# Linear attention and a gated feed-forward layer: loads of v and DMA transposes apart, the last block's addition ahead of its seventh product, new lists for blocks 2 to 8

## The chip, the cores and the metric

The kernel runs on one core of one Trainium2 chip. The metric is the device time of a run in microseconds (us), of which the median of three runs is given. A profile is one execution that the hardware profiler recorded; it has a time of its own, and all stretches, gaps and durations below are measured from the start of its span.

The engines are called PE or TensorE (matmul; PEld is its weight load), DVE or VectorE, ACT or ScalarE, POOL or GpSimd, and SP or SyncE, which here only issues DMAs. L12 is line 12 of the kernel before.

## What is computed

Attention without a score matrix: softmax of q over the head dimension, softmax of k over the sequence, and two small products. The result is laid out as 4608 rows of 512 and goes through a feed-forward layer with a GELU gate.

```python
def _attn_ref(q, k, v):             # each (8, 8, 576, 64): batch, heads, sequence, head dimension
    q_s = softmax of q over its last axis
    k_s = softmax of k over the sequence
    kv = np.einsum('bhsd,bhse->bhde', k_s, v)
    return np.einsum('bhsd,bhde->bhse', q_s, kv)

def _moe_ref(x, w_gate, w_val, w_out):   # x (4608, 512), w_gate and w_val (512, 1536), w_out (1536, 512)
    gelu = 0.5 * g * (1.0 + erf(g / sqrt(2)))     # g = x @ w_gate
    return (gelu * (x @ w_val)) @ w_out
```

## The kernel before, in words

**Blocks.** One batch element is one block. Of its 576 rows 512 are worked through with the block; the 64 that are left of each element are gathered in `xtr` and make up a block of their own, number 8, which comes ahead of the last one. So the order is 0 to 6, 8, 7. While block b goes through its feed-forward layer, the attention of the next one is made beside it.

**Attention of one block.** q, k and v come by two DMAs each on SyncE's queue (`load`, L180). ScalarE makes the exponentials of q and k (`exp`, L223, instruction at L227). VectorE sums those of q and takes reciprocals (`norm_pair`, L250), and GpSimd multiplies (L265). The normalised `eq` is transposed by a DMA on SyncE's queue (`unit_td`, L415, DMA at L418) into `eqt`. v is cast to 16 bits by ScalarE or GpSimd (`cast_v`, L232). TensorE makes kv from the exponentials of k and v (`unit_kv4`, L361), VectorE normalises it (`kv4_norm`, L374), TensorE multiplies it with `eqt` (`unit_x4`, L454), and ScalarE and VectorE copy one half each of the result to `xt` (`x4_out`, L484). From block 3 on, `eq` has one buffer: the exponentials of the next q are written to where the transpose reads.

**Feed-forward layer.** From block 2 on all its matrix products are done by Strassen's scheme with seven products of half size. `product_gv` (L660) makes one product of the first layer for one of six column groups (0, 1, 2, 6, 7, 8), value and gate together: four matmuls of 128x256. `product` (L739) makes one of the seven products of the second layer, twelve matmuls of 128x256. Which sums of x, h and the weights they need is in `sum_x` (L653), `sum_h` (L616) and `sum_w1` (L644). Several products share a PSUM bank: product 1, then 6, then 7, then 4 of the second layer add up in `psA`, product 5, then 3, in `psC`, and product 2 in `psB`. Between two of them another engine must have read the bank: y1 is read from `psA` after product 1, y2 after product 6, y5 from `psC` after product 5. The additions b+ (`psB` and y1), c+ (`psC` and y2) and a+ (`psA` and y5) make three quarters of the block's output, and the last quarter is `psA` after product 4.

**What sets the order.** Nothing is scheduled by the compiler. `PROG` (L675) holds a list of entries for each block from 2 on, and `play` (L817) issues them one after another; every engine works through its own in that order. The entries that the text speaks of:

- `0P1`: product 1 of the first layer, column group 0 (the digit in front). `0c`: ScalarE copies product 1 to the bank of the other sum. `0s2`, `0s5`: scale a bank's content into SBUF (ScalarE; with d, VectorE). `0a2`, `0a5`: VectorE's additions. `0g2`, `0g4`: GELU on ScalarE. `0m2`, `0m4`: VectorE's multiplication with the gate. `0u`: GELU of the other half. `0U`: its multiplication on GpSimd, `0Ud` on VectorE.
- `s01p`, `s21d`: sums of h, on GpSimd (p) or VectorE (d). `x0d`, `x1p` and so on: sums of x. `z`: the same for the last block. `w`: sums of weights.
- `O1:03`: product 1 of the second layer, its steps 0 and 3. `O7`: product 7. `y1a`, `y2d`: y1 by ScalarE, y2 by VectorE. `b+`, `c+`, `a+`: the additions. `yea`: the last quarter, by ScalarE. c+ and ye are each followed by a store of 512 KB.
- `lq`, `lk`, `lv`: the loads for two blocks on. `Eq`, `Ek`: exponentials of q and k. `NA`, `NB`: sums and reciprocals. `M0` to `M3`: GpSimd's multiplications. `t`: the transpose. `tr`: a small transpose for the rows of block 0 in block 8. `V0a` to `V3p`: casts of v. `K`, `k`, `X`, `Xa`, `Xd`: kv, its normalisation, the product with `eqt`, and its two copies. `TE`, `TG`: ScalarE's table for the exponential or for GELU.
- `<` in front of an entry means that it belongs to the block before, `>` to the one after.

A DMA waits on SyncE's sequencer for what it needs, and all DMAs behind it on that queue wait with it.

**The last block.** Its output banks are split in two, one for each 128 rows. `finish_last` (L962) makes product 7 for the first half, its addition (L965), the same for the second half, stores the second half's columns, makes product 4 for the first half (read by ScalarE, L970, and stored from ScalarE's queue), and for the second half (read by VectorE, L973, and stored from SyncE's). It is called at `O7`; `c+` of that block, with its 512 KB store, comes behind it in the list.

Of the kernel before, what the change touches and what calls it, by code (L numbers as in the profile page):

```python
# [18 lines left out]
def kernel(  # L19
# [640 lines left out]
    def product_gv(i, ps, xt, k, first):  # L660
        lo, hi = slice(k * P, (k + 1) * P), slice((k + NO // 2) * P, (k + NO // 2 + 1) * P)
        xs = xs_b[xt is st.get((B - 1, "xt"))]
        for t, w, nm in ((0, wv_sb, "v"), (1, wg_sb, "g")):
# [9 lines left out]


    PROG = {  # L675
        2: ("lk lq lv 6P1 0P1 <x0p 2P1 w81d 0P5 <x1d 6P5 <x3d 6c w82d 6P2 0c <x2d 6P6 w71d 0s5 0P6 6s5 0P3 6P3 6s2 "
            "w72p 6g2 0P2 NB 0s2 6P7 6m2 w83p 0P7 0g2 6a2 1P1 2c 0a2 2P2 M3 1P5 0a5 1c 0P4 0m2 2g2 1P2 0u 6a5 M2 1P6 "
            "0g4 2P5 6u 2P6 1s5 0U 6P4 1g2 NA 1P3 1s2 0m4 2m2 1P7 2s5 6U 1m2 7P1 2s2 2P3 6g4 1a2 s01p 2P7 1a5 7P5 6m4 "
            "1u 1P4 2a2 M0 8P1 7c 2a5 7P6 7s5 w73d 7P2 w74d 8c 8P5 7s2 1Ud 7P3 1g4 w84d 8P6 s02d 2u 7P7 s04d 8s5 2P4 "
            "7a2 8s2 8P3 7a5 2U 8P7 2g4 1m4 8P2 7u 8a2 7P4 7g2 M1 t O1:03 8g2 >>lr 8a5 8P4 7g4 2m4 7m2 O1:1 8u O1:4 "  # L680
            "7U 8m2 O1:25 8g4 7m4 K 8m4 8U O2 s11d TE s21d y1a s23d s22d O5 s24d s12d k O6 Eq b+ s14p y5a O3:03142 "
            "s03p y2a >NB X s13d O7 Xa Xd O3:5 x0d"),
        3: ("0P1 <x1d 6P1 <a+ 0P5 <O4 <c+ <x3p <Ek lk 6c 0c 6P5 M2 lq 0s5 6P6 NA 0P3 6s5 M3 0P6 <yea 6s2d 0P2 6P3 "
            "<x2p 0s2d 6P2 <TG 0P7 0a2 0g2 1P1 M1 6a2 <V3a 6P7 6g2 <V2p 0a5 7P1 1c 6m2 0P4 0u 1P5 6a5 7c 1P6 0Ud 0g4 "
            "1P2 6u 1s5d 6P4 1s2 7P2 6Ud 1P3 0m2 1P7 0m4 7g2 6g4 7P5 7m2 s01p 7P6 <V1a 1a5 2P1 7s5 6m4 1P4 M0 7s2 1a2 "
            "7P3 1g2 s02d 7P7 1g4 1m2 8P1 2c s04d 1m4 2P6 <V0a 2P5 lv 7a5 8c O1:03 7a2 2s2 O1:1 t 7P4 1u 8P6 7u 2P7 "
            "1Ud 2s5 8P5 8s2 2P3 7g4 2a5 8P7 7U 8s5 2P2 2a2 8P2 s11p 8P3 2g2 8a5 7m4 8P4 8g2 2P4 s13p 2u 8a2 O1:4 8g4 "
            "K 8m2 2g4 8m4 O2 2m4 8u 2U 2m2 8Ud s21d O1:25 TE s23d O5 s12d s14d y1a s22d O6 k b+ s24p y5d X Eq >lq "
            "s03p O3:03142 y2a V3p Xd O7 Xa V0a"),
        4: ("6P1 NA 0P1 <x0d <O3:5 <x1d 6P5 0P5 <a+ <Ek lk <O4 0c <c+ <x3p 6c 0s5d <V2p 0P6 6P6 <TG 0P3 M0 <yea NB "  # L690
            "6P2 6s2 0P2 0s2d <x2p 1P1 6g2 0a2 0P7 0g2 1P5 6s5d M3 1c 0m2 6P7 6m2 6P3 0a5 1P2 M1 0P4 6a5 1s5 7P1 0u "
            "6a2 1P6 M2 0g4 1g2 6P4 7c 1P3 1s2d 0U 7P5 6u 6g4 1P7 1a2 7P2 7s5 6m4 7P6 6U 0m4 2P5 1m2 7g2 2P1 7m2 <V1a "
            "s01p lv 7P3 1a5 7s2 8P1 2c 2s5d 7P7 t s02p 1u 1P4 7a2 2P6 8c 7a5 s03p 2P3 s04d 8P6 7u 8P5 1Ud 2s2 7P4 "
            "8s2 2P7 2a2 1g4 7U 2P2 8s5 1m4 7g4 8P7 2a5 8P2 2g2 s11p 8P3 2u 8a5 2P4 8g2 2m2 s13p 8P4 7m4 K 2g4 8a2 "
            "8g4 2m4 O1:03 2U 8m2 8u O1:1 O1:4 k O1:25 8m4 X TE 8U O2 y1d s21d s22d Xa s23d O5 s12d s14d"),
        5: ("0P1 <Eq <O6 <Xd lq <x2d <Er <x0d 0c <x1d 6P1 <x3d <y5a <s24d 0P5 <O3:03142 6c <y2a <O7 NB <V0a 0s5d 0P6 "
            "<b+ M2 6P6 6P5 <V1p <Ek <O3:5 lk 6P2 0s2 NA 0P2 0P3 <a+ 0P7 <c+ <TG M1 <O4 0g2 6g2 0a2 0m2 6s2 6m2 M3 "
            "1P5 6s5 0a5 6P3 0P4 0u M0 1s5d 6P7 1P1 0g4 6a2 7P1 <yea 6a5 7P5 1c 6P4 7c Rr 1P6 0m4 7P6 6g4 0Ud 7P2 6u "
            "6m4 1P3 7s2 1P2 1s2d 7g2 7P7 7s5 6U 1a2 2P1 1g2 7m2 1P7 1m2 <V2a s01p 8P1 2c 7P3 1a5 2P6 Rm 8c 8P5 7a5 "
            "1u s03d 1P4 7P4 <V3a 7a2 lv 2P5 1g4 2s2d 8P6 8s5 t 2P7 >tr 1Ud 7u 1m4 2P2 7g4 8P3 8s2 2s5d 8P7 2g2 2a5 "  # L700
            "7U 8P2 7m4 2P3 8a2 2P4 s11p 8g2 O1:03 8a5 2m2 8P4 2g4 s12p O1:1 2a2 8u O1:4 8m2 K 8g4 2m4 2u 8m4 O1:25 "
            "8U O2 2Ud TE s21d s13d y1a O5 s22d s02d s04d s24d O6 s14d y5d Eq O3:03142 k V0a b+ V3a s23d X y2a O7 Xa "
            "Xd O3:5 x0d"),
        6: ("6P1 0P1 <a+ 0P5 <x1p <c+ 6P5 <Ek <O4 6c <x3p 6s5 NB 0c 6P6 <x2p 0s5 0P6 <yea 0P2 <V2p 6P2 0s2 NA 6P3 M3 "
            "0P3 6s2d 1P1 <TG 6a2 0P7 6g2 M2 6P7 0g2 0a2 6m2 7P1 1c 0m2 1P6 M1 <V1a 7P5 0a5 7c 1P2 6a5 0u 7P2 M0 t "
            "1s2d 1P5 1g2 0P4 7g2 0Ud 1m2 6P4 6u 1P7 0g4 1s5d 1P3 6g4 0m4 7P6 7s5 6U 1a5 2P1 6m4 7P3 7s2 1a2 s01p 2P5 "
            "2c 7m2 7P7 1u 2P6 s03p 2s5d 8P1 1P4 7a5 2s2 2P7 1U 7a2 8c 8P5 8P6 7u 2a5 2P3 8s5 2P2 7Ud 8s2 2P4 1g4 2a2 "
            "8P7 2g2 1m4 8P3 s11p 2g4 7P4 2u 8a5 O1:03 s13p O1:1 7g4 8a2 K 2m4 8u 2m2 O1:4 2U 7m4 8P2 O1:25 8Ud s21d "
            "8P4 8g2 s02d O5 s04d 8g4 s22d s12d y1a O6 k 8m2 y5a 8m4 s24d O2 s14d s23d y2a O7 b+ X O3:03142 a+ O4 Xa "
            "Xd x0d >z0d"),  # L710
        8: ("0P1 <x1d <x3d 6P1 <x2d <O3:5 z1d 6P5 0c 0P6 6c <c+ 6P6 0P5 <yed 0s2 6P2 6s5 6s2d 0P7 6P3 6g2 0s5d 6P7 "
            "6m2 7P1 6a2 0P3 1P1 0a5 7c 0P2 0a2 7P6 1c 7P2 6a5 0g2 1P6 0m2 0u 0P4 6u 7P5 0Ud 7g2 6P4 1s2 6Ud 0g4 1P5 "
            "s01d 1P2 7m2 7s5 6g4 0m4 7P3 1s5 2P1 7s2d 1g2 1P7 s02p 7a2 1P3 2c 6m4 2P5 1m2 2P2 z2d 8P1 1a2 7P7 1a5 "
            "8P5 8c 2P6 2s5d 1u s03d 1P4 8P6 7a5 2s2 8P2 8s5d 7u 2P3 8s2 2P7 1Ud 8g2 7P4 1g4 2a2 2g2 8P7 7U"),
        7: ("0P5 <7g4 <2a5 <1m4 <2P4 <8P3 <8a5 <s11p <8P4 <8m2 <2g4 <7m4 0P1 <s13p <O1:03 <8a2 <2m4 <O1:1 <O1:4 0c "
            "<2m2 6P1 <8g4 <z3p 0P2 <8m4 <2u <O1:25 <8u <O2 <2Ud 0s5 0g2 <8Ud <s21d 6c 0P6 <s12d <y1a 0m2 <O5 <s22p "
            "0s2 <s24d <O6 <s14d <s04d <y5a 0P3 <O3:03142 <y2d <s23d 6P2 <b+ <O3:5 <O7 6P5 6P6 <a+ 0P7 6s5 <O4 <c+ "
            "6s2 6g2 0a2 0a5 1P1 6m2 6P7 6P3 <yed 1c 0P4 0u 6a5 7P1 1P6 0g4 6a2 1P5 0Ud 7c 6P4 6u 1s2d 7P6 1s5 1P2 "
            "6Ud 6g4 7P5 s01d 0m4 1P7 s02d 7P2 6m4 7s5 1P3 1a5 7P3 7g2 8P1 7s2 s04p 1a2 1g2 1P4 7m2 7P7 s03d 8c 2P1 "
            "7a2 1u 8P6 1g4 8P5 7a5 2c 1m2 7P4 1m4 7u 1U 2P5 8s2 8s5d 2P6 7g4 8P7 7Ud 2s5 8P3 7m4 2s2 s11d 8P2 2P7 "  # L720
            "8a5 2P3 8g2 8a2 s12p 8P4 2a5 2P2 8u 2P4 8g4 s14p 2a2 O1:03 8m2 2g2 8m4 O1:1 2g4 O1:4 2m2 O2 8U 2u 2m4 "
            "2Ud s21d O1:25 O5 s22p y1d s24d O6 y5d s23d O3 b+ y2a s13d O7 c+ O4 a+ yed"),
    }
    live = {}

# [91 lines left out]
    def play(b, x):  # L817
# [30 lines left out]
        if k is not None and x[1] == "P":  # L848
            i = int(x[2])
# [53 lines left out]
        elif x[0] == "O":  # L903
# [2 lines left out]
            nm = {2: "psB", 5: "psC", 3: "psC"}.get(i, "psA")  # L906
            first = nm not in t
            t.setdefault("yo", first and [yop.tile([P, 2, C], f32, name="yo", tag="yo") for _ in range(2)])
            if last and i == 7:
                finish_last(b, t["psA"], t["yo"][1], t["y5"])  # L910
            elif not last or i != 4:
                if first:
                    t[nm] = ([big([P, 256], f32, nm, True) for _ in range(2)] if last else
                             [big([P, 2, 256], f32, nm, True)])
                product(i, t[nm] if last else [t[nm][0][:, j] for j in range(2)], first, js=js)
# [7 lines left out]
                drop("psA")  # L923
                store_rows(b, 1, t["yo"][1])
        elif x[1:] == "+":
            if x[0] != "a" or not last:
                nm, y, half, col = {"b": ("psB", "y1", 0, 0), "c": ("psC", "y2", 0, 1), "a": ("psA", "y5", 1, 1)}[x[0]]
                for r, src in parts(nm):
                    add(t["yo"][half][:, r, c[col]], src, t[y][:, r], 1.0 / _H_SCALE)
                let_row(t[y])  # L930
                if x[0] != "a":
                    drop(nm)
                if x[0] == "c":
                    store_rows(b, 0, t["yo"][0])
# [27 lines left out]
    def finish_last(b, ps, yo, s5):  # L962
        for t in range(2):
            product(7, ps, False, (t,))
            nc.vector.scalar_tensor_tensor(  # L965
                out=yo[:, t, 256:], in0=ps[t], scalar=1.0 / _H_SCALE, in1=s5[:, t],
                op0=ALU.mult, op1=ALU.add)
        store(nc.sync, yo[:, 1, 256:], b, 3, 4, 256, 512)
        product(4, ps, False, (0,))
        nc.scalar.activation(out=yo[:, 0, 0:256], in_=ps[0], func=ACTF.Copy, scale=1.0 / _H_SCALE)  # L970
        store(nc.scalar, yo[:, 0], b, 2, 3)
        product(4, ps, False, (1,))
        nc.vector.tensor_scalar(out=yo[:, 1, 0:256], in0=ps[1], scalar1=1.0 / _H_SCALE,  # L973
                                scalar2=None, op0=ALU.mult)
        store(nc.sync, yo[:, 1, 0:256], b, 3, 4, 0, 256)
# [198 lines left out]
```

The softmax here doesn't subtract the row's maximum and nothing guards it: scores larger than these inputs give would overflow.

## Time and profile before

| | |
|---|---|
| Median of three runs | 292.63 us (292.55 to 294.7) |
| The run that was profiled | 292.85 us, span 290.9 us |
| TensorE clock granted | 0.999 of full speed |
| Busy, TensorE / VectorE / ScalarE / GpSimd | 278.2 / 246.9 / 210.5 / 151.1 us |
| Moved by DMA | 51.74 MB, mean 178 GB/s |
| Block 2's first product | at 82.4 us |
| Last matmul's end | at 285.6 us |

A row of the timeline has the start, the length, the engine and line, the instruction, its tiles as out<-in with their shapes, and how many such instructions were merged. In brackets stands how long the engine was idle ahead of it and what ended that. A row with SPq is a DMA's issue on SyncE's sequencer, and its length is the time that the issue took there; the landing of its data comes later and is told by the answers on a tile or a line ("DMA to landing"). A row of the waits has the engine and line that waited, the engine and line that it waited for, the sum in us, the number of times, and the longest one. A row of busy times by stage has the stage's length, then the busy time and number of instructions of PE, PEld, DVE, ACT and POOL, the granted clock, the share of DMA time and GB/s.

### The profile page before, as it was taken

Reading aid. Unit: us, or ns where it says so; the run is one execution under the profiler, and the core shown is the slowest. Engines: PE = TensorE matmul, PEld = TensorE weight load, DVE = VectorE, ACT = ScalarE, POOL = GpSimd, SP = SyncE. Lnnn points to the kernel's source line nnn. Section 1 sums busy time; section 2 is a strip of 40 time slices with the busy share of each in tenths; the row PEclk is TensorE's granted clock in tenths of the full one; section 3 lists DMA queues with packets and bytes.
Section 4 is the critical chain, followed back from the end, with each engine's and each line's share of the span. In section 5 each row is a group of like instructions: output and inputs, shape, how many; then the busy total and the mean of one; then the engine's idle time right before and its main releaser. Section 6 shows DMA issues by size and latency. Waiting matters only on the chain.

```text
span 290.9 us, 6711 instructions
## 1 busy us (share of the span) xinstructions
PE 278.2 (96%) x2581; PEld 216.7 (75%) x2581; DVE 246.9 (85%) x488; ACT 210.5 (72%) x369; POOL 151.1 (52%) x138
## 2 busy tenths in 40 slices
PE   3999999999999999999999999997999999999992
PEld 1544445445888888888888788886888888888882
DVE  2854888877999998989999999997989799869972
ACT  3773367785798989988988998779984476626820
POOL 1567746986449647454799165515872003601530
PEclk9999999999999999999999999999999999999999
DMA  6999999999049354983869176571330030006003
GB/s 211 375 380 388 400 393 390 368 341 234 13 156 372 117 100 140 326 187 76 233 238 241 21 220 247 150 114 74 100 66 2 1 146 0 2 0 147 1 2 144
DMA packets 54623, 51.74 MB, mean 178 GB/s; under 512 B 18496, under 2 KB 50496, under 8 KB 54592
## 3 DMA queue, kind: packets, MB, share of 16 engines
q1 hardware_dynamic: 52864, 49.49, 55.2%
q10 hardware_dynamic: 1728, 1.84, 2.0%
q8 instruction: 20, 0.33, 0.4%
q14 instruction: 11, 0.09, 0.1%
HBM read 37.75 MB, written 9.44 MB: 162 GB/s over the span
## 4 chain that ended last, share of the span: by engine, by line
PE 79%; DMA 8%; DVE 4%; POOL 4%; issue 2%; ACT 1%; DVEq 0%; POOLq 0%; ACTq 0%
PE psa L670 21%; PE psA L749 11%; PE psc L670 11%; PE psg L511 7%; PE psv L511 7%; DMA eqt<-eq 6%; PE psC L749 6%; PE psb L670 5%; PE psy L579 4%; PE psB L749 3%; DMA qt<-in_q_dram 2%; POOL eq L265 2%; PE psa L749 1%; POOL xs L658 1%; DVE rq L255 1%
## 5 line engine op out<-in xcount | busy, mean ns | idle before, releaser
L670 PEld LDWEIGHTS <-wgv_sb 128*128 128x128 f16 x672 | 65.7, 98 | 7.8
L265 POOL TENSOR_TENSOR eq<-eq,rrq 128x640 f16<-128x640 f16 (+1 forms) x27 | 34.8, 1304 | 20.4 <-DVE rrq L257 16.9
L749 PEld LDWEIGHTS <-ht 128*128 128x128 f16 x384 | 37.0, 98 | 8.1 <-issue 3.3
L670 PE MATMUL psa<-xs,wgv_sb 128*128 128x256 f16 x288 | 40.7, 273 | 0.0
L511 PEld LDWEIGHTS <-wgv_sb 128*128 128x128 f16 x192 | 18.6, 98 | 21.9 <-issue 0.2
L858 ACT COPY psb<-psa 128x512 f32<-128x512 f32 x42 | 24.1, 585 | 8.2 <-PE psa L670 8.1
L511 PE MATMUL psv<-xt,wgv_sb 128*128 128x512 f16 x96 | 26.6, 379 | 0.0
L511 PE MATMUL psg<-xt,wgv_sb 128*128 128x512 f16 x96 | 26.6, 379 | 0.0
L886 POOL TENSOR_TENSOR ht<-eq 128x512 f16<-128x512 f32 x12 | 16.0, 1332 | 19.2 <-ACT eq L884 15.7
L516 ACT ACTIVATE gl<-psg 128x512 f32<-128x512 f32 x24 | 13.8, 597 | 16.7 <-PE psg L511 15.6
L517 DVE SCALAR_TENSOR_TENSOR ht<-psv,gl 128x512 f16<-128x512 f32 x24 | 16.0, 685 | 9.6 <-PE psv L511 8.0
L227 ACT ACTIVATE ek<-kt 128x1280 f16<-128x1280 f32 (+1 forms) x11 | 19.3, 1761 | 5.6 <-DMA kt<-in_k_dram 3.9
L227 ACT ACTIVATE eq<-qt 128x2560 f16<-128x2560 f32 (+2 forms) x10 | 18.4, 1863 | 5.4 <-DMA qt<-in_q_dram 2.9
L749 PE MATMUL psA<-tw,ht 128*128 128x256 f16 x168 | 20.5, 272 | 1.7 <-ACT gl L839 1.7
L839 ACT ACTIVATE snq<-psc 128x512 f32<-128x512 f32 x29 | 17.4, 603 | 5.8 <-PE psc L670 5.6
L255 DVE TENSOR_REDUCE rq<-eq 128x20 f32<-128x1280 f16 (+1 forms) x12 | 17.1, 1429 | 4.7 <-ACT eq L227 4.7
L670 PE MATMUL psb<-xt,wgv_sb 128*128 128x256 f16 x144 | 20.8, 273 | 0.0
L670 PE MATMUL psa<-xt,wgv_sb 128*128 128x256 f16 x144 | 20.6, 273 | 0.0
L749 PEld LDWEIGHTS <-sh 128*128 128x128 f16 x192 | 18.7, 98 | 2.5 <-DVE gl L766 0.3
L626 POOL TENSOR_TENSOR sh<-sh,ht 128x512 f16<-128x512 f16 x6 | 7.1, 1175 | 25.1 <-DVE ht L876 19.9
L839 ACT ACTIVATE snq<-psa 128x512 f32<-128x512 f32 x31 | 18.5, 601 | 1.8 <-PE psa L670 1.8
L874 ACT ACTIVATE gl<-psb 128x256 f32<-128x256 f32 x42 | 15.8, 384 | 5.3 <-PE psb L670 4.9
(192 smaller groups left out, 717.6 us busy)
## 6 DMA issues: line engine op xcount, KB each, us to landing
out_dram<-yo SPq DMA_DIRECT2D x15, 512.0 KB, 4.4
kt<-in_k_dram SPq DMA_DIRECT2D x7, 640.0 KB, 8.0
vt<-in_v_dram SPq DMA_DIRECT2D x7, 640.0 KB, 5.3
qt<-in_q_dram SPq DMA_DIRECT2D x7, 640.0 KB, 7.0
qt<-in_q_dram SPq DMA_DIRECT2D x8, 512.0 KB, 8.0
wost<-in_moe_w_out_dram SPq DMA_DIRECT2D x6, 512.0 KB, 7.9
kt<-in_k_dram SPq DMA_DIRECT2D x6, 512.0 KB, 7.8
vt<-in_v_dram SPq DMA_DIRECT2D x6, 512.0 KB, 6.5
```

The source lines that it names most:

```text
L227: nc.scalar.activation(out=dst[:, n0:NC, h0 * D:h1 * D].rearrange(o, d=D, **({"t": 2} if b >= QUAD else {})), in_=heads(tiles[(nm, b)], b, ...
L255: nc.vector.reduce_sum(rq, e, axis=mybir.AxisListType.X)
L265: (nc.gpsimd if eng == "pool" else nc.vector).tensor_tensor(out=e, in0=e, in1=rrq.unsqueeze(-1).to_broadcast((P, n, 2, D)), op=ALU.mult)
L511: nc.tensor.matmul(ps, w[:, ci, fi * P:(fi + 1) * P], xt[:, ci, :], start=(ci == 0), stop=(ci == HP - 1))
L516: nc.scalar.activation(out=gl, in_=psg, func=ACTF.Gelu)
L517: nc.vector.scalar_tensor_tensor(out=ht[:, fi, :], in0=psv, scalar=_H_SCALE, in1=gl, op0=ALU.mult, op1=ALU.mult)
L670: nc.tensor.matmul(ps[:, t], a, x, start=(first and t == 0 and c == 0), stop=(c == 1), skip_group_check=True)
L749: nc.tensor.matmul(ps[t], a, w, start=(first and j == js[0] and (t == ts[0] or ps[t].tensor is not ps[ts[0]].tensor)), stop=(j == js[-1]), ...
L839: nc.scalar.activation(out=dst, in_=src, func=ACTF.Copy, scale=scale)
L858: nc.scalar.copy(out=t[f"b{k}"], in_=t[f"a{k}"])
L874: nc.scalar.activation(out=gl, in_=t[ps][:, 1], func=ACTF.Gelu)
L886: (nc.vector if side == "dve" else nc.gpsimd).tensor_tensor(out=ht[:, k:k + NO // 2 + 1:NO // 2, 256:512], in0=cc[:, :, 0], in1=cc[:, :, 1 ...
```

## The change

All seven lists are new. The set of entries of each block is nearly the same, so both kernels issue the same matmuls (5164 rows of TensorE's program in each); what differs is the order, and for some entries the engine, by their last letter. Counted over all lists:

| Entries | before | after |
|---|---|---|
| sums of h on VectorE / GpSimd | 56 / 28 | 65 / 19 |
| second halves' multiplication (U) on VectorE / GpSimd | 21 / 21 | 24 / 18 |
| scalings s2, s5 on ScalarE / VectorE | 60 / 24 | 61 / 23 |
| y1, y2, y5, ye on ScalarE / VectorE (without the last `yed`, which does nothing) | 19 / 8 | 20 / 7 |
| sums of x for the blocks up to 8 on VectorE / GpSimd | 16 / 8 | 16 / 8 |
| casts of v on ScalarE / GpSimd | 11 / 5 | 9 / 7 |

The order of the DMAs on SyncE's queue changes in blocks 2 to 5. For block 3 (entries `lv`, `t`, `lk` and their stores) and those that follow:

```
block 3   before: out, k, k, q, q, out, v, v, transpose, q, q
          after:  q, q, out, out, transpose, k, k, v, v
block 4   before: k, k, out, out, v, v, transpose
          after:  out, transpose, out, v, v, q, q, k, k
block 5   before: q, q, k, k, out, out, v, v, transpose, small transpose
          after:  q, q, out, out, v, v, transpose, k, k, small transpose
```

In the code, `a+` of the last block takes over what `O7` did there, so that `c+` can stand ahead of it:

```diff
-            if last and i == 7:
-                finish_last(b, t["psA"], t["yo"][1], t["y5"])
-            elif not last or i != 4:
+            if not last or i in (1, 2, 3, 5, 6):
...
         elif x[1:] == "+":
-            if x[0] != "a" or not last:
+            if x[0] == "a" and last:
+                finish_last(b, t["psA"], t["yo"][1], t["y5"])
+            else:
```

The end of the last block's list:

```diff
-2Ud s21d O1:25 O5 s22p y1d s24d O6 y5d s23d O3 b+ y2a s13d O7 c+ O4 a+ yed
+2Ud s21d O1:25 s12d O5 s14d s22d y1a s24d s13d O6 b+ y5a s23d O3 y2d O7 c+ O4 a+ yed
```

The ends of blocks 2, 3 and 5 and the entries that follow, cut to what the prediction speaks of:

```diff
 block 2, then the start of 3
-O6 Eq b+ s14p y5a O3:03142 s03p y2a >NB X s13d O7 Xa Xd O3:5 x0d | 0P1 <x1d 6P1 <a+ 0P5 <O4
+O6 Eq >lq b+ y5a k s24d X s04d s13d y2a O3:03142 s23d O7 Xa Xd V2a x2d x0d O3:5 x1d | 0P5 6P5 <a+ 0P1
 block 3, then the start of 4
-O6 k b+ s24p y5d X Eq >lq s03p O3:03142 y2a V3p Xd O7 Xa V0a | 6P1 NA 0P1 <x0d <O3:5
+O6 k b+ s24p y5d X Eq s03p O3:03142 Xa s13p Xd | 6P1 0P1 <y2d <x0d <O7 <Ek <x1p 0P5
 block 5
-O6 s14d y5d Eq O3:03142 k V0a b+ V3a s23d X y2a O7 Xa Xd O3:5 x0d
+O6 s23d k Eq s04d X y5a O3:03142 y2d Xa O7 Xd x2d x0d
```

In block 5 the entries ahead of the transpose read `1a5 2P6 Rm 8c 8P5 7a5 1u s03d 1P4 7P4 <V3a 7a2 lv 2P5 1g4 2s2d 8P6 8s5 t` before, and `7P2 <V0a lv 2P1 7a2 2P5 1a5 M3 7P7 0m4 2c 1P4 1m2 7g2 s02d 8P1 1u 7m2 2P6 1g4 7a5 8P5 8c 7P4 t` after.

## The prediction

> **What bounds the kernel now.** I read the page first, then the waits of TensorE, then the timeline at the two places where TensorE stands still, last the busy times by stage.
>
> ```profile
> PE 278.2 (96%) x2581; PEld 216.7 (75%) x2581; DVE 246.9 (85%) x488; ACT 210.5 (72%) x369; POOL 151.1 (52%) x138
> ```
> ```profile
> PE pswarm L503 <- ACT warm L1004: 4.9, 1, 4.9
> PE psA L749 <- ACT gl L839: 1.7, 1, 1.7
> PE psxr L462 <- DMA eqt<-eq: 0.3, 1, 0.3
> PE psa L749 <- DVE yo L770: 0.2, 1, 0.2
> ```
>
> TensorE is the bound, and its waits name all that can be won inside: 1.7 and 0.3 us lie in blocks that the change touches (4.9 and 0.2 lie ahead of block 2). The 1.7 us has this history, first on ScalarE, then on TensorE, then in the answer on the transpose of that stage:
>
> ```profile
> 191.29 0.58 ACT L839 ACTIVATE gl<-psA 128x512 f32<-128x512 f32 x1
> 193.81 2.34 ACT L227 ACTIVATE eq<-qt 128x2560 f16<-128x2560 f32 x1 [1.94 <-DMA eqt<-eq]
> 196.06 1.34 ACT L205 CAST v<-vt 128x640 f16<-128x640 f32 x2
> 197.29 0.58 ACT L839 ACTIVATE gl<-psA 128x512 f32<-128x512 f32 x1
> ```
> ```profile
> 195.64 0.60 PE L462 MATMUL psx<-eqt,kv 64*64 64x512 f16 x8
> 197.93 0.27 PE L749 MATMUL psA<-tw,ht 128*128 128x256 f16 x1 [1.69 <-ACT gl L839]
> ```
> ```profile
> 183.71 1.35 SPq L183 DMA_DIRECT2D vt<-in_v_dram  x2
> 185.16 5.30 SPq L418 DMA_TRANSPOSE eqt<-eq  x1
> ...
> 208.70 3.10 SPq L418 DMA_TRANSPOSE eqt<-eq  x1
> ```
> ```profile
> DMA to landing us min/median/max: 8.6/8.6/8.6
> ...
> DMA to landing us min/median/max: 4.9/4.9/4.9
> ```
>
> The exponentials of the next q (L227) overwrite `eq`, which the transpose still reads, so ScalarE stands 1.94 us until the transpose has landed at 193.8. Behind it in ScalarE's order are two casts of v and y2 (L839 at 197.29), and the seventh product adds into the PSUM that y2 must have read. The transpose went out right behind the two halves of a v load and took 8.6 us; the one at 208.70, with no load near it, took 4.9. The same pairing at 125.93 and 153.27 took 8.5 and 8.0 by the same view; the second is the 0.3 us wait of TensorE.
>
> The tail is the other place. These are VectorE's last rows and SyncE's:
>
> ```profile
> 283.63 0.42 DVE L965 SCALAR_TENSOR_TENSOR yo<-psA,gl 128x256 f32<-128x256 f32 x1 [1.30 <-PE psA L749]
> ...
> 285.61 0.42 DVE L973 TENSOR_SCALAR yo<-psA 128x256 f32<-128x256 f32 x1 [0.91 <-PE psA L749]
> 285.95 0.74 DVE L842 SCALAR_TENSOR_TENSOR yo<-psC,gl 128x256 f32<-128x256 f32 x2
> ```
> ```profile
> 284.74 2.56 SPq L589 DMA_DIRECT2D out_dram<-yo  x3
> ```
>
> The additions of the third product (L842) stand behind those of the seventh and the scaling of the fourth, though VectorE sat idle 1.30 us ahead of 283.63. So the 512 KB store of half of the block's rows is issued last, at 286.7, and lands 3.0 us later; the span ends 1.1 us after that, at 290.9.
>
> Last, the busy times of 82.4 to 193 us, blocks 2 to 5:
>
> ```profile
> 82.40:193.00 110.60, 110.29 (x1169) 96.68 (x1167) 104.61 (x210) 99.05 (x184) 68.42 (x59) 1.00 0.67 189
> ```
>
> VectorE (third) is 104.6 of 110.6 us busy: the second resource is nearly as full as the first.
>
> **What the Trainium skill says.** TensorE: Matmul & The Clock Gate, section Back-to-back issue gap, gives N/2.4 + 2.5 ns for warm matmuls, 109 ns at 256 columns; the chain of waits has 12 of them in 1.31 us, so this trace agrees and TensorE's own work can't shrink. DMA: Bandwidth & Descriptors, section Queues, rings and completion order, says that each of the 16 engines consumes one queue's ring in order; the 8.0 to 8.6 us behind a v load against 4.9 alone agree. The same page, Anatomy of one DMA, puts about 2.0 us plus bytes/436e3 on a transfer (for another issue path): 2.3 us for 128 KB, 3.2 for 512; the trace has 2.1 and 3.0.
>
> **The change part by part.** First the constant: both sets of lists hold the same TensorE work. Counted with the chain's durations (four matmuls of a product of L670 0.437, a product of L749 1.31, kv and x about 0.75 each) it is 200 us in each; started at 82.4, this and the waits reach the 285.6 of the trace. So I use the running sum of products as a ruler and place the other entries on it.
>
> *The loads of v.* SyncE's order changes in three stages. In blocks 3 and 4 the two v loads move from right ahead of the transpose to behind it (with the k load, or with stores, q and k between). In block 5 they remain next ahead of the transpose in the queue, but the last cast that they wait for stands 3.0 us earlier on the ruler, so they should issue at about 183.7 - 3.0 = 180.7. The transpose there waits for its last multiplication on GpSimd (M3, 1.27 us), which moves down to about the same place; I take the transpose at 182.1 at the earliest. At 8.0 to 8.6 us it lands by 190.7, at worst by 192; ScalarE is free for L227 from 191.87. So its 1.94 us go, and with them TensorE's 1.7. In block 4 the transpose issues near 149 on the ruler and is needed at 162: the 0.3 goes. SyncE's k load behind it and the small transpose behind that are needed only at 197 and 224: hidden under products.
>
> *Three new handovers.* y2 of block 5 moves to VectorE, so the seventh product no longer waits for ScalarE; but y5 moves to ScalarE behind L227, and the last of product 3 adds into what y5 reads. L227 from 191.9 takes 2.34, y5 0.6: 194.9, against product 3 at 194.6 on the ruler: 0 to 0.35 us lost. In block 3 the next block's first two products now come ahead of the seventh; they need xt, whose copies on ScalarE (0.26 + 1.08) start when x ends at 136.5: 137.9, against 137.6: 0 to 0.3 lost. In block 2 the fifth product of the next block comes first, needing x0 on VectorE at 110.1, which I find ready at 110.0: 0. Sum 0 to 0.65; I take 0.3, as the trace of before shows no wait in such places where my sums give 0.1 or 0.2.
>
> *The lists otherwise.* Counted by engine: nine sums (0.42) and three multiplications (0.69) go from GpSimd to VectorE, and two scalings (0.68) on balance from VectorE to ScalarE: VectorE +3.8 + 2.1 - 1.4 = +4.5 us, GpSimd 9 x 1.16 + 3 x 1.3 less two casts of 0.72 = -12.9. In blocks 2 to 5 VectorE's share is +2.4 of 6.0 us idle. It stays below TensorE, and in stretches of 10 us on the ruler its fullest one falls from 12.0 to 11.3 us of summed durations (which overlap by about 7%): cost 0.
>
> *The tail.* The additions need product 3, done at 282.9: VectorE does them 283.0 to 283.7, in its idle time. L965 moves from 283.63 to 283.70 and ends at 284.12; the fourth product's first half wants its bank at 284.08: 0.1 lost. The 512 KB store issues at 283.8 and lands by 287 to 288. L973 ends at 286.1, its 128 KB store issues at 286.2 and lands 2.1 later, at 288.3; plus 1.1 is 289.4. Gain 290.9 - 289.4 = 1.4 to 1.5; I take 1.4, between 1.1 (stores share the engines) and 1.5.
>
> Sum: -1.7 - 0.3 + 0.3 - 1.4 = -3.1. The profiled span is 290.9 and goes to 287.8; the run that was profiled took 292.85 and the median is 292.63, so the time goes to 292.6 - 3.1 = 289.5.
>
> **The rivals.** *The transpose of block 5 stays late.* For: its v load is still the transfer just ahead of it. If M3 or the casts slip by 2 us, it lands after 192.5 and L227 waits again. Then only tail and 0.3 are won: 292.6 - 1.7 + 0.3 = 291.2. That is the change not doing what it says. Against: 1.2 to 1.8 us of room.
>
> *The handovers eat it.* ScalarE's or VectorE's order at the ends of blocks 2 to 5 costs about 0.7 us in each of four places instead of 0.3 in all: 289.5 + 2.5 = 292.0. For: VectorE is 95% busy there and y work moved; against: those stages had no wait of TensorE before.
>
> *VectorE becomes the bound (slower).* Place: blocks 2 to 5 and the last two. Its order is fixed, and a late addition holds a PSUM bank that the next product needs. It decides where the added work passes the idle time of its stretch. If all 4.5 us come out as TensorE waits while the tail and 2.0 are won, 292.6 - 3.4 + 4.5 = 293.7, and up to 296 if GpSimd's later results hold VectorE too. Against: 2.4 added to 6.0 idle.
>
> **How the numbers follow.** Forecast 0.62, own range 288.1 (every gain, no handover) to 290.8; transpose late 0.18 (291.2); handovers 0.10 (292.0); VectorE 0.10 (293.7 to 296). Median run 289.6, rounded up from 289.5 for the half that lean to more handovers. The range for 8 in 10 takes in the first three: 288.1 to 292.6. About 1% (2.9 us) is what a measurement of this kernel can tell from no change; the boundary at 289.7 cuts the forecast's range, so faster by over 1% gets 0.45, within 1% 0.45, slower by over 1% 0.10.
>
> **What would show it.** Right: no wait of L227 for the transpose near 192; transposes of blocks 3 and 4 land in under 7 us; no 1.7 us gap of TensorE ahead of a seventh product; L842 on psC ahead of L965, and a 128 KB store as the last one. Wrong: TensorE waiting for VectorE or ScalarE at L670 or L749 in places that had none, VectorE busy above 98% in blocks 2 to 5, or the block 5 transpose landing after 192.

## The result, and the profile after

The kernel after takes 288.88 us (median of four runs, 288.76 to 288.97) against 292.59 us for the kernel before (292.52 to 294.7, four runs): a ratio of 0.9856, with a 95% interval of 0.9811 to 0.99. By the medians that is 3.7 us less, a ratio of 0.9873. The ratio with the interval isn't that of the medians: the one run before at 294.7 draws it down and makes the interval wide. The forecast was 289.6, a gain of 3.0.

The profiled execution has a span of 286.9 us (before: 290.9). Two lines from the head of its page:

```profile
span 286.9 us, 6704 instructions
...
PE 277.9 (97%) x2581; PEld 216.4 (75%) x2581; DVE 248.3 (87%) x497; ACT 209.8 (73%) x370; POOL 137.9 (48%) x128
```

The waits of TensorE, the whole answer:

```profile
PE pswarm L503 <- ACT warm L1004: 4.9, 1, 4.9
PE psa L749 <- DVE yo L770: 0.2, 1, 0.2
```

The 1.7 and the 0.3 are gone and no wait of their size has come in their place. The two that are left lie ahead of block 2.

Now block 5. SyncE's rows with the v load and the transpose, and the transpose's landing:

```profile
180.27 1.34 SPq L183 DMA_DIRECT2D vt<-in_v_dram  x2
181.72 5.37 SPq L418 DMA_TRANSPOSE eqt<-eq  x1
```
```profile
DMA to landing us min/median/max: 8.9/8.9/8.9
```

The load still stands right ahead of the transpose, and the transpose takes no less than before (8.9 us against 8.6). It is only issued 3.4 us earlier (185.16 before), so it has landed at 190.6. The load can go 3.4 us earlier because the cast that it waits for ends at 180.2 here and at 183.6 before. The last multiplication that the transpose waits for (M3) ends at 181.40, so the load keeps a ready transpose waiting for 0.3 us only. The timeline from there, ScalarE and TensorE:

```profile
190.95 0.58 ACT L839 ACTIVATE gl<-psA 128x512 f32<-128x512 f32 x1
...
191.43 2.33 ACT L227 ACTIVATE eq<-qt 128x2560 f16<-128x2560 f32 x1
...
193.66 0.59 ACT L839 ACTIVATE gl<-psC 128x512 f32<-128x512 f32 x1
...
194.21 0.60 PE L462 MATMUL psx<-eqt,kv 64*64 64x512 f16 x8
...
194.74 1.27 PE L749 MATMUL psC<-wo_sb,s 128*128 128x256 f16 x10
...
195.84 1.47 PE L749 MATMUL psA<-tw,ht 128*128 128x256 f16 x12
```

L227 has no wait in brackets any more. Behind it y5 (L839 on psC) has ended at 194.25, and product 3, which adds into that bank, starts at 194.74, when the products ahead of it are done: the new handover has half a us to spare. The seventh product (psA, 195.84) follows without a gap.

The tail, the last rows of VectorE and SyncE, and the landing of the last store of SyncE:

```profile
280.40 0.76 DVE L842 SCALAR_TENSOR_TENSOR yo<-psC,gl 128x256 f32<-128x256 f32 x2 [0.50 <-PE psC L749]
281.18 3.03 SPq L589 DMA_DIRECT2D out_dram<-yo  x3
281.22 0.42 DVE L965 SCALAR_TENSOR_TENSOR yo<-psA,gl 128x256 f32<-128x256 f32 x1
281.88 0.42 DVE L965 SCALAR_TENSOR_TENSOR yo<-psA,gl 128x256 f32<-128x256 f32 x1 [0.24 <-PE psA L749]
...
283.22 0.42 DVE L973 TENSOR_SCALAR yo<-psA 128x256 f32<-128x256 f32 x1 [0.91 <-PE psA L749]
```
```profile
DMA to landing us min/median/max: 2.2/2.2/2.2
```

The additions of the third product (L842 on psC) now stand ahead of L965, in time that VectorE had idle. The 512 KB store is the first of the three on SyncE's row, at 281.18, and what is issued last, at 283.7, is 128 KB. From the end of the last matmul (283.2) to the end of the span it is 3.7 us; before it was 5.3.

So the 4.0 us between the spans lie thus: 1.6 in the tail; 2.1 between block 2's first product and the last matmul (203.2 us before, 201.1 after); and 0.3 ahead of block 2 (its first product starts at 82.11 instead of 82.42), where the change has touched nothing. I put that down to chance: over all fourteen traces, with the old lists and with the new, that start lies between 82.1 and 82.4 in no order.

Two small gaps of TensorE were in no step. One of 0.25 us at 215, in block 6, is gone. A new one of 0.27 us stands in block 3 at 118.3 (both are read from start to start, that is from the starts of TensorE's rows less the time that the matmuls between take, and are too short for the answer on the waits). There product 4 of group 0 needs a bank that an addition of VectorE (L842 on psa) still has to read, and the addition is queued behind a multiplication (L876):

```profile
117.27 0.41 DVE L876 SCALAR_TENSOR_TENSOR ht<-psb,gl 128x256 f16<-128x256 f32 x1
...
117.60 0.68 DVE L842 SCALAR_TENSOR_TENSOR eq<-psa,snq 128x512 f32<-128x512 f32 x1
```

Last, the busy times of blocks 2 to 5:

```profile
82.40:193.00 110.60, 110.49 (x1169) 96.59 (x1167) 104.72 (x214) 99.41 (x185) 65.68 (x57) 1.00 0.62 189
```

VectorE (third) has four more instructions in this stretch than before, but 104.7 us of busy time against 104.6; GpSimd has 65.7 against 68.4.

### The profile page after: what moved, and what is told of

Read it like the earlier page. It is cut to its first block, busy times and chain, and to the rows that moved or that the text cites. A ratio compares the mean times of both kernels' runs of the same rounds, so it can differ in the third digit from the quotient of the medians.

```text
span 286.9 us, 6704 instructions
## 1 busy us (share of the span) xinstructions
PE 277.9 (97%) x2581; PEld 216.4 (75%) x2581; DVE 248.3 (87%) x497; ACT 209.8 (73%) x370; POOL 137.9 (48%) x128
## 4 chain that ended last, share of the span: by engine, by line
PE 91%; DVE 5%; ACT 1%; issue 1%; ACTq 1%; DVEq 0%
PE psa L670 24%; PE psc L670 12%; PE psA L749 12%; PE psg L511 7%; PE psv L511 7%; PE psC L749 6%; PE psb L670 6%; PE psy L579 4%; PE psB L749 3%; PE pswarm L503 2%; PE pskv L368 1%; PE psa L749 1%; DVE rq L255 1%; ACTq L183 1%; DVE yo L770 1%
## 5 line engine op out<-in xcount | busy, mean ns | idle before, releaser
L670 PEld LDWEIGHTS <-wgv_sb 128*128 128x128 f16 x672 | 65.7, 98 | 8.0 <-issue 0.3
L858 ACT COPY psb<-psa 128x512 f32<-128x512 f32 x42 | 24.2, 583 | 8.3 <-PE psa L670 8.1
L839 ACT ACTIVATE snq<-psc 128x512 f32<-128x512 f32 x35 | 20.6, 602 | 5.7 <-PE psc L670 5.6
L227 ACT ACTIVATE ek<-kt 128x1280 f16<-128x1280 f32 (+1 forms) x11 | 19.2, 1758 | 5.9 <-DMA kt<-in_k_dram 4.2
L670 PE MATMUL psb<-xt,wgv_sb 128*128 128x256 f16 x144 | 21.6, 273 | 0.0
L227 ACT ACTIVATE eq<-qt 128x2560 f16<-128x2560 f32 (+2 forms) x10 | 18.4, 1861 | 2.6 <-DMA qt<-in_q_dram 2.6
L886 POOL TENSOR_TENSOR ht<-cc 128x512 f16<-128x512 f32 x12 | 15.3, 1274 | 9.1 <-ACT cc L884 8.8
L876 DVE SCALAR_TENSOR_TENSOR ht<-psb,gl 128x256 f16<-128x256 f32 x42 | 17.1, 412 | 1.8 <-ACT gl L874 1.6
L874 ACT ACTIVATE gl<-psa 128x256 f32<-128x256 f32 x42 | 16.1, 385 | 3.4 <-PE psa L670 2.9
```

What stands on the lines that cost most here:

```text
L227: nc.scalar.activation(out=dst[:, n0:NC, h0 * D:h1 * D].rearrange(o, d=D, **({"t": 2} if b >= QUAD else {})), in_=heads(tiles[(nm, b)], b, ...
L670: nc.tensor.matmul(ps[:, t], a, x, start=(first and t == 0 and c == 0), stop=(c == 1), skip_group_check=True)
L839: nc.scalar.activation(out=dst, in_=src, func=ACTF.Copy, scale=scale)
L858: nc.scalar.copy(out=t[f"b{k}"], in_=t[f"a{k}"])
L874: nc.scalar.activation(out=gl, in_=t[ps][:, 1], func=ACTF.Gelu)
L876: nc.vector.scalar_tensor_tensor(out=ht[:, k if x[2] == "2" else k + NO // 2, 0:256], in0=t[ps][:, 0], scalar=_H_SCALE, in1=t["g" + ps], o ...
```

## The experiments

Twelve kernels were run, on three chips. Each ratio is to the kernel before, on the same chip, with its 95% interval. In the diffs a line is a stretch of a list.

### The tail and the lists, each alone

`tail_alone` has the old lists with only the addition moved; `after_old_tail` has the new lists with the addition where it was.

```diff
 tail_alone, in the kernel before
-if last and i == 7: finish_last(...)
+if x[0] == "a" and last: finish_last(...)
```

> The kernel before with the old lists; only the last block's two additions of the third product and their 512 KB store go ahead of the seventh product's additions. Theory (the tail is worth 1.4 to 1.6 us and adds up with the rest): 0.995, so about 291.1 us; the last matmul ends at 285.6 as before, and the span ends 3.7 to 3.9 us after it instead of 5.3. Rival (the large store, now in flight together with the last small ones, slows them as much as it is earlier, and the lists alone won the time): within 0.3 us of before.

> The changed lists with the old place of the addition behind the seventh and fourth products: the lists alone. Theory (parts add up): before less 2.1 to 2.6 us, ratio 0.992, with the 5.3 us from last matmul to end of span back. Rival (the parts overlap: the gain of the lists needs the new tail, or the other way round): less than 1.5 us or more than 3.2 us of gain.

`tail_alone` took 291.3 us, ratio 0.9945 (0.9932 to 0.9959), 1.6 us less. Its trace has the gap ahead of 197.9 still (1.5 us), and from the last matmul to the end 3.8 us. `after_old_tail` took 290.38 us, ratio 0.9917 (0.9904 to 0.9931), 2.6 us less; its 512 KB store goes out last, at 284.62, and lands at 287.64. The product of the two ratios is 0.9862, and the kernel after has 0.9856. By the medians the two gains are 1.6 and 2.6 us against 3.7 for both, by the profiled spans 1.6 and 2.2 against 4.0. To within half a us the two halves of the change add up.

### Block 5: earlier, elsewhere, or another engine

Three edits of the kernel before, each in block 5's list alone.

```diff
 v_earlier_5: the last cast and the load earlier, the load still the DMA ahead of the transpose
-<V2a s01p ... 7P4 <V3a 7a2 lv 2P5 1g4 2s2d 8P6 8s5 t
+<V2a <V3a lv s01p ... 7P4 7a2 2P5 1g4 2s2d 8P6 8s5 t
 v_behind_5: the load behind the transpose
-<V3a 7a2 lv 2P5 1g4 2s2d 8P6 8s5 t 2P7
+<V3a 7a2 2P5 1g4 2s2d 8P6 8s5 t lv 2P7
 y2_vector_5: y2 by VectorE
-b+ V3a s23d X y2a O7 Xa Xd
+b+ V3a s23d X y2d O7 Xa Xd
```

> The kernel before with one edit: in block 5 the last cast of v that the v load waits for, and the load with it, stand some 3 us earlier in the list; the load stays right ahead of the transpose. Theory (what counted is when the transpose is issued, not what stands ahead of it): transpose issued near 182.5, still 8 to 9 us to land, by 191.5; the exponentials of q don't wait, TensorE's 1.7 us ahead of the seventh product go; ratio 0.994. Rival (the neighbourhood of load and transpose is what costs, as the change is described): the wait stays, ratio above 0.998.

> The kernel before with one edit: in block 5 the load of v stands behind the transpose in SyncE's queue. Theory of earliness: the transpose no longer waits for the casts ahead of the load, is issued before 184 and lands by 189 to 190, so the exponentials don't wait; but v itself lands near 194 to 195 and the two casts that stand ahead of y2 on ScalarE wait for it: 0.3 to 1.0 of the 1.7 us stay; ratio 0.995 to 0.998. Rival (keeping the load away is all that is needed): the full 1.7 us, ratio 0.994.

> The kernel before with y2 of block 5 read by VectorE instead of ScalarE, the transpose left late. Theory (the transpose has to come earlier; behind y2 the copies of xt stand in the same queue): the seventh product no longer waits, but the next block's first product does, about 1.1 of the 1.85 us stay; ratio 0.9975. Rival (the handover alone was the cost): all 1.7 go, ratio 0.994.

`v_earlier_5` took 291.27 us, ratio 0.9948 (0.9936 to 0.9961). The loads went out at 181.75 and the transpose at 183.21, both 2.0 us earlier than in the kernel before (the edit was meant to give 3); it took 9.0 us and landed at 192.2, L227 waited 0.3 us, and the gap of TensorE shrank from 1.85 us (start to start) to 0.24. Being earlier is enough, with the load in the same neighbourhood.

`v_behind_5` took 291.03 us, ratio 0.9939 (0.9927 to 0.9952). Its rows on SyncE's queue, and the landing of its transpose:

```profile
177.44 4.45 SPq L418 DMA_TRANSPOSE eqt<-eq  x1
183.72 1.36 SPq L183 DMA_DIRECT2D vt<-in_v_dram  x2
```
```profile
DMA to landing us min/median/max: 6.1/6.1/6.1
```

The transpose went out at 177.44, where the kernel before has it at 185.16. So it had been ready for at least 7.7 us, and what held it was the v load ahead of it, which stood on SyncE's sequencer until ScalarE's casts had emptied `vt` (the load's time, 183.7, didn't change). Two rows of the kernel before, SyncE's stores ahead of the load and the cast that the load waited for:

```profile
173.01 4.28 SPq L589 DMA_DIRECT2D out_dram<-yo  x2
```
```profile
182.93 0.71 ACT L205 CAST v<-vt 128x640 f16<-128x640 f32 x1
```

GpSimd's multiplications for this transpose had ended at 175.6 there and the stores' issue at 177.3; the load went out 0.07 us after the end of that cast. The transpose itself is 2.5 us faster in `v_behind_5` (6.1 against 8.6), and it is issued 7.7 us earlier. Each of the two alone is more than the 1.94 us that ScalarE waited. The edit makes both, and only the second was also tried without the first, by `v_earlier_5`. I had expected that the v load would now be late and leave a wait of 0.3 to 1.0 us; it was no later, because its time is set by the casts, and no wait was left at the end of block 5.

`y2_vector_5` took 292.05 us, ratio 0.9979 (0.9972 to 0.9986), as expected. (One of its 22 runs took 1029 us, from a cause that I don't know; the ratio is without it.) The seventh product no longer waits, but the transpose is as late as ever and ScalarE as blocked, so TensorE waits in four shorter gaps, from the seventh product to the next block's first ones: 0.20, 0.43, 0.38 and 0.35 us in place of 1.85. The last three are waits for ScalarE's copies.

The opposite edit, on the kernel after: the last cast and the load later, to right ahead of the transpose.

```diff
 after_v_late_5, block 5
-7P2 <V0a lv 2P1 7a2 ... 8P5 8c 7P4 t
+7P2 2P1 7a2 ... 8P5 8c <V0a lv 7P4 t
```

> The changed kernel with block 5's cast and load of v put back to about 3.5 us later, right ahead of the transpose. Theory (lateness costs in the new lists too, now by y5 on ScalarE behind the exponentials): transpose lands near 193.5, TensorE waits 1.5 to 2.0 us ahead of the last part of product 3, ratio to the kernel before 0.991 to 0.993. Rival (the move of y2 to VectorE has made that stage safe from a late transpose): under 0.5 us, ratio below 0.988.

It took 292.8 us (291.0 to 293.41), ratio 0.999 (0.9971 to 1.001): nearly the whole gain of the change is gone, about twice what I expected. ScalarE's rows, and then TensorE's:

```profile
191.34 0.58 ACT L839 ACTIVATE gl<-psA 128x512 f32<-128x512 f32 x1
194.54 2.34 ACT L227 ACTIVATE eq<-qt 128x2560 f16<-128x2560 f32 x1 [2.62 <-DMA eqt<-eq]
196.79 0.58 ACT L839 ACTIVATE gl<-psC 128x512 f32<-128x512 f32 x1
```
```profile
194.64 0.62 PE L462 MATMUL psx<-eqt,kv 64*64 64x512 f16 x8
197.42 2.29 PE L749 MATMUL psC<-wo_sb,s 128*128 128x256 f16 x10 [2.15 <-ACT gl L839]
199.50 2.04 PE L749 MATMUL psA<-tw,ht 128*128 128x256 f16 x12
```

The transpose went out at 185.78, so L227 waits 2.6 us, y5 behind it is late, and product 3 waits for y5 where the kernel before had product 7 wait for y2. The new list gave the place behind L227 to another reader; it didn't make the place safe. The rest is in the lengths: the ten matmuls of 197.42 take 2.29 us, where the kernel after has 1.27. The busy times of the stretches around the gap, with the granted clock third from the end of a row:

```profile
190.00:194.00 4.00, 4.00 (x45) 3.56 (x38) 3.83 (x11) 1.91 (x3) 0.34 (x1) 1.00 1.37 164
194.00:197.40 3.40, 1.26 (x22) 0.61 (x20) 2.44 (x6) 2.86 (x3) 0.00 (x0) 0.98 0.89 268
197.40:200.70 3.30, 3.28 (x16) 2.29 (x16) 1.19 (x3) 2.81 (x4) 0.81 (x1) 0.51 0.35 105
200.70:204.00 3.30, 3.30 (x33) 2.94 (x32) 2.39 (x4) 2.57 (x5) 0.35 (x1) 1.00 0.00 0
```

For the 3.3 us behind the gap the clock was half of full speed, and 16 matmuls started where 33 do in the next 3.3: 1.6 us on top of the wait. The runs show it too: ten of the fourteen have a mean clock of 0.991 to 0.993 and take 292.7 to 293.4, the other four have 0.999 to 1.0 and take 291.0 to 291.6. The four are 2.1 to 2.8 us above the kernel after, about what the wait alone is.

### Blocks 3 and 4, both ways

`v_behind_34` is the kernel before with the loads behind the transposes in blocks 3 and 4; `after_v34_ahead` is the kernel after with the loads, and the cast that they need, right ahead of them.

```diff
 v_behind_34, block 3 (block 4 in the same way)
-2P5 lv 7a5 8c O1:03 7a2 2s2 O1:1 t 7P4
+2P5 7a5 8c O1:03 7a2 2s2 O1:1 t lv 7P4
 after_v34_ahead, block 3 (block 4 in the same way, with V3p)
-8P1 1g4 M2 t 2P6 1u 7a5 2P5 <V1p 8c ... s12p lv 2m2
+8P1 1g4 M2 <V1p lv t 2P6 1u 7a5 2P5 8c ... s12p 2m2
```

> The kernel before, with the loads of v behind the transpose in blocks 3 and 4 only. Theory: the transposes of both go out earlier, because SyncE no longer stands at the load's wait for the casts of v ahead of them; block 4's lands before it is needed and TensorE's 0.5 us there goes, block 3's was no wait of TensorE: 0.4 to 0.6 us in all, ratio 0.998. Rival (the transposes wait for GpSimd, and are late anyway): no change.

> The changed kernel with the loads of v (and the cast that each waits for) right ahead of the transpose in blocks 3 and 4, so all three loads stand ahead. Theory (in these lists the transposes go out 2 to 6 us sooner than they must, so the neighbourhood is free): block 3's lands near 134 instead of 130.4, block 4's near 157 to 158 instead of 153.7, both before they are needed: 0 to 0.3 us, ratio to the kernel before 0.9856 to 0.987. Rival (keeping v away is what the change lives on): 0.8 us or more, ratio above 0.988.

`v_behind_34` took 292.46 us, ratio 0.9993 (0.9984 to 1.0002): within its interval no gain. The transposes took 4.9 and 6.6 us instead of 8.5 and 8.0, and TensorE's gap at 161.4 (0.5 us start to start) is gone, but block 5's has grown from 1.85 to 1.98. Its transpose landed at 193.4 instead of 193.8, so that of the 0.5 us won ahead of it 0.1 was handed to that wait.

`after_v34_ahead` took 290.18 us (289.83 to 290.85), ratio 0.991 (0.9893 to 0.9926): 1.3 us more than the kernel after, where I had expected next to nothing. A wait of TensorE in block 3, and ScalarE's rows there:

```profile
PE psa L670 <- ACT psb L858: 1.3, 1, 1.3
```
```profile
134.73 2.34 ACT L227 ACTIVATE eq<-qt 128x2560 f16<-128x2560 f32 x1 [0.38 <-DMA eqt<-eq]
...
139.54 2.34 ACT L227 ACTIVATE ek<-kt 128x2560 f16<-128x2560 f32 x1 [1.34 <-DMA kt<-in_k_dram]
```

The transpose's own landing costs ScalarE 0.4 us. What costs 1.3 is the k load: the exponentials of k wait for it, and behind them stands ScalarE's copy (L858) that TensorE waits for. The size is that of the rival, but the path isn't the one that either side had. SyncE's rows tell why:

```profile
124.68 1.34 SPq L183 DMA_DIRECT2D vt<-in_v_dram  x2
126.12 6.54 SPq L418 DMA_TRANSPOSE eqt<-eq  x1
132.71 1.29 SPq L183 DMA_DIRECT2D kt<-in_k_dram  x2
```

The transpose goes out 2.4 us later than in the kernel after (123.68) and holds the sequencer for 6.5 us instead of 3.1, so the k load goes out at 132.71 instead of 126.82. Block 4's transpose was late in the same way (9.2 us) and cost nothing.

### Is anything left over for the rest of the lists?

`old_lists_345_tail` is the kernel before with the three loads behind their transposes and the tail, and nothing else. `after_m2_later_3` is the kernel after with block 3's multiplication behind the addition that product 4 waits for.

```diff
 after_m2_later_3, block 3
-0a5 7c <x3p 6m2 7P2 0g2 0P4 6a5 1c
+0a5 7c <x3p 7P2 0g2 0P4 6a5 6m2 1c
```

> The kernel before with four edits and nothing of the new lists: the load of v behind the transpose in blocks 3, 4 and 5, and the last block's addition ahead of its seventh product's. Theory (these four are all that the change won; the rest of the new lists is neutral): before less 1.9, 0.5 and 1.6, so 0.9865 and within 0.5 us of the changed kernel. Rival (the even load on VectorE in the new lists carries part of it): at least 0.8 us slower than the changed kernel, ratio above 0.9885.

> The changed kernel with one of VectorE's multiplications of block 3 put behind an addition that TensorE waits for, at the one place where the new lists made TensorE wait (0.27 us at 118.3). Theory (VectorE runs there without a gap for 7 us, and its order decides): the 0.27 us go in the trace, the time is 0.2 to 0.3 us less than the changed kernel's, which is about what can be told apart. Rival (the bank of that product is held by something else): the gap stays.

The first took 289.14 us (289.04 to 289.28), ratio 0.9878 (0.9862 to 0.9894), 3.45 us less. Four small edits give all but 0.3 us of what the new lists give, and the intervals don't tell that 0.3 from nothing. In its trace the one gap of TensorE that is left in blocks 2 to 6 is that of 0.25 us in block 6. The second took 288.6 us, ratio 0.986 (0.9845 to 0.9874); its gap at 118.3 is gone from the trace, but its time can't be told from that of the kernel after.

### How much room VectorE has

The kernel after with 10 and with 30 additional sums on VectorE (128x512, both operands from the weights, a result that nothing reads), spread over blocks 2 to 6, `D` in the lists:

```diff
+"D": lambda: nc.vector.tensor_tensor(out=warm, in0=wo_sb[:, 0], in1=wo_sb[:, 1], op=ALU.subtract)
```

> The changed kernel with 10 more instructions of 0.42 us on VectorE, two in each of blocks 2 to 6 (a difference of two weight rows written to a tile that nobody reads): 4.2 us. Theory (VectorE has 5.9 us idle in blocks 2 to 5 and more after, but in single stretches of some us none at all): 0.3 to 1.0 us slower than the changed kernel. Rival (the idle time takes it all): under 0.2 us. Other rival (VectorE is the bound already): 3 to 4 us.

> The same with 30 such instructions, one for each column group of blocks 2 to 6: 12.6 us, more than VectorE's idle time there. Theory (past the idle time every us counts): 5 to 8 us slower than the changed kernel. Rival (durations overlap, VectorE is not near its limit): under 2 us.

Ten took 295.75 us (294.8 to 296.77), ratio 1.0105 (1.0071 to 1.0138), some 7 us more than the kernel after. Thirty took 305.5 us, ratio 1.0436 (1.0407 to 1.0466), 17 us more. Both far exceed what I expected. Part of it is that the sums weren't of the size I took: the ten took 8.4 us together, not 4.2, and the thirty 23.2. The answer on them, and two of them on VectorE's timeline; then GpSimd's:

```profile
L960 DVE TENSOR_TENSOR warm<-wo_sb x10: 409/825/1411, 87.0 to 210.4; 128x512 f16<-128x512 f16 x10
```
```profile
87.03 1.41 DVE L960 TENSOR_TENSOR warm<-wo_sb 128x512 f16<-128x512 f16 x1
...
88.97 0.77 DVE L960 TENSOR_TENSOR warm<-wo_sb 128x512 f16<-128x512 f16 x1
```
```profile
86.90 1.26 POOL L265 TENSOR_TENSOR eq<-eq,rrq 128x640 f16<-128x640 f16 x1
88.12 1.33 POOL L651 TENSOR_TENSOR kt<-wgv_sb,kt 128x512 f16<-128x512 f16 x1
89.42 1.44 POOL L265 TENSOR_TENSOR eq<-eq,rrq 128x640 f16<-128x640 f16 x1
```

The sum at 87.03 ends at 88.44, the one at 88.97 at 89.74: each 0.3 us after the GpSimd instruction that was running when it began (88.16 and 89.45), as though it had waited for that one and then run. GpSimd's two later rows are stretched too (1.33 and 1.44 us, where the kernel after has 1.16 and 1.26). Of the ten sums, the eight that began beside a GpSimd instruction took 0.53 to 1.41 us; the two that began beside none, or in the last 0.06 us of one, took 0.41. Each of the eight ended 0.28 us after that instruction. The same holds in `vector_30` for 22 of its 30 sums (0.45 to 1.51 us, all ended 0.28 us after the GpSimd instruction beside which they began); the other eight took 0.41. It isn't so for every instruction of VectorE: the additions with one operand in PSUM (L842, 128x512) took 0.63 to 0.69 us in `vector_10`, the 54 that began beside a GpSimd instruction and the 48 that didn't. The Trainium skill, SBUF — State Buffer, section SBUF: two separate sides, says that VectorE, in an operation with two operands in SBUF, and GpSimd take a shared pair of ports as an exclusive lock for a whole instruction. All these durations agree; the ports themselves are in no trace.

Three of the waits of TensorE in `vector_10`:

```profile
PE psa L670 <- DVE cc L842: 2.2, 2, 1.7
PE psc L670 <- DVE ht L876: 1.6, 1, 1.6
PE psA L749 <- DVE yo L842: 0.7, 1, 0.7
```

8.4 us of VectorE's time became 6 us of the kernel's (294.8 to 294.9 in the two runs at full clock), and 23.2 became 16 (304.6 to 304.8). The two other runs of `vector_10`, with mean clocks of 0.991 and 0.993, took 296.6 and 296.8. In blocks 2 to 5 VectorE's busy share of 95% has the look of 5% of room, 5.9 us. At these places most of the additional time came out in the kernel's, since by the waits above an addition or multiplication that comes late holds a bank of PSUM that a product needs at a fixed place. Other places for the sums weren't tried.

## Why the prediction was right

**The transpose of block 5 (-1.7): right in place and size.** It was forecast to issue at 182.1 at the earliest and land by 190.7; it issued at 181.72 and landed at 190.6, and L227 started at 191.43 without a wait. `v_earlier_5` alone gives 1.7 us and `v_behind_5` 1.9. The rule that the step used, that an earlier cast makes an earlier load and an earlier transpose, held in both runs that moved the cast. What was weak is the account of why it had been late: the text lays the weight on the 8.0 to 8.6 us behind a load (the 8.6 is 2.5 us more than in `v_behind_5`), and the larger part is the 7.7 us that the transpose stood ready behind the load's wait.

**Block 4 (-0.3): right in the trace, smaller in the time.** The transpose issued at 147.2 (forecast: near 149) and landed in 6.5 us, block 3's in 6.7, and the gap is gone. Alone, blocks 3 and 4 give 0.13 us, with an interval that holds nothing at all.

**New handovers (+0.3): 0 at the places named.** y5 behind L227 had half a us to spare, and blocks 2 and 3 show no wait. A gap of 0.27 came at another place, on VectorE, and 0.25 went away at a third; neither was foreseen, and they cancel. That block 4's 0.3 and the 0.3 here had opposite signs in the sum, and both came to little, is luck for the forecast.

**VectorE and GpSimd (0): right for this change, on a weak argument.** VectorE's busy time rose by 1.4 us in all and by 0.1 in blocks 2 to 5, not by 4.5 and 2.4. Part of the difference is that durations overlap, in blocks 2 to 5 by 11% (117.4 us of durations in 104.5 us of busy time before), not by the 7% that the text has for one stretch; added up simply, they rose by 2.2 and 0.9. But "2.4 added to 6.0 idle" isn't what made it safe: ten sums at other places cost 6 to 7 us. The room was far thinner than that argument says. I take it that the rival that made VectorE the bound was held off by where the instructions stand, not by their sum; that this came out at 0 owes as much to luck as to the working.

**The tail (-1.4): -1.6.** `tail_alone` gives 1.6. The last store was issued 0.5 us after the last matmul's end, where the sum had 0.6; its landing (2.2 us) and the 1.1 behind it came as worked out. The 0.1 that the sum lost at the fourth product's bank isn't the tail's: the last 24 matmuls take 2.87 us against 2.80 before, but 2.88 in `after_old_tail` too, and 2.81 in `tail_alone`. The rest of the 0.2 is within the interval.

**The sum.** -3.1 was forecast, -3.7 measured; the steps as the runs give them, taken singly, are -1.7 to -1.9, -0.1 and -1.6, that is -3.4 to -3.6. The Trainium skill, TensorE: Matmul & The Clock Gate, section Back-to-back issue gap, gives the formula that the prediction used for a single matmul by itself, and other figures for a stream; that twelve matmuls in a stream keep to it here is what the 1.31 us of the trace show. Of the rivals, the late transpose is what `after_v_late_5` makes by hand, and it costs more than the 1.7 us that its figure of 291.2 allowed for, since the clock falls behind it.

## What to carry to other kernels

On a queue that is worked through in order, a DMA that waits for a buffer to come free also holds what is ready behind it: look for how long the one behind had been ready, not only for how long it took. Order such a queue by when the transfers can go out, and put a transfer whose issue is long behind those that others wait for soon. A second engine that is 95% busy may have far less room than its idle sum: count where its instructions stand.

## What the runs showed of the hardware

- **A wait of TensorE can cost more than its length.** Behind the 2.15 us of `after_v_late_5` the granted clock was 0.51 for 3.3 us in the profiled run, and by their mean clocks in ten of fourteen runs. Behind the 1.7 us of the kernel before it is rare: of 51 runs of it that stand beside four of the experiments one had a mean clock below 0.995 (0.991), and took 295.02 us where the others took 292.2 to 293.64. With the 1.8 us of `v_behind_34` it was one of 22 (0.99, 294.47 us), and in `vector_10`, with waits of 1.7 and 1.6 us, two of four; where in these runs the clock fell isn't on record. The Trainium skill, TensorE: Matmul & The Clock Gate, section What's actually happening, puts the fall to half the clock after an idle window of about 3.4 us; here a gap of 2.15 us was enough, with eight small 64x512 and eight 64x64 matmuls ahead of it. In the 3.4 us from 194.00 on TensorE was busy for 1.26. Which of the two, the wait or the small matmuls, brings it under was not tried.
- **The issue of a transpose takes longer behind a load.** It held SyncE's sequencer for 3.1 us at 123.68 in the kernel after, 5.4 us behind a load at 181.72, and 6.5 us behind one in `after_v34_ahead`, where the k load behind it went out right at its end. Behind two stores, in `v_behind_5`, it was 4.5 us.
- **A 128x512 sum on VectorE with both operands in SBUF took up to 1.51 us instead of 0.41 where it began beside a GpSimd instruction.** All 30 such sums of `vector_10` and `vector_30` ended 0.28 us after that instruction, unless they began in its last 0.06 us. So a sum put on VectorE beside a busy GpSimd isn't to be counted at the duration that it has alone.
